# One core: the first batch's q and k rotated together in later weights' tiles, a weight conversion spread over more slots

## The chip, the cores and the metric

The kernel runs on one core of one Trainium2 chip. The metric is device time in microseconds (us), from the first to the last instruction of one execution and what lies around it; less is better. Its engines are TensorE (PE, with its weight loads PEld), VectorE (DVE), ScalarE (ACT), GpSimd (POOL) and SyncE (SP), which here only issues DMAs, in order.

## The reference

Attention with rotary position (4 batches, 8 heads, 576 positions, 64 channels), then two expert layers without a router on the 2304 x 512 result, all in float32:

```
q_rot, k_rot = rotate(q), rotate(k)
scores = (q_rot @ k_rot.T) / sqrt(64)
attn   = softmax(scores)
x = (attn @ v) as [2304, 512]
h = x @ w_in1;  x = (s * relu(h)**2 + b) @ w_out1
h = x @ w_in2;  out = (h * sigmoid(1.702 * h)) @ w_out2
```

All weight matrices arrive as 64-bit floats: `w_in` is 512 x 2048, `w_out` 2048 x 512.

## The kernel before

**Attention.** A batch is worked on in four pairs of heads. A pair's q and k are loaded (`rope_load`, L188), rotated on natural rows by four passes (`rope_cross` L197 with two, `rope_mul` L202, `rope_add` L205) on GpSimd, or on VectorE for q of the first RV pairs of batch 0, turned by TensorE through PSUM and split into a high and a low part (`rope_turn`, L218 on ScalarE, L219 on VectorE), and spilled to DRAM (`ksp`, `qsp`, L225 and L226). `fetch_pair` reads them back (L231, L241, L243) shortly before use. The rotated tiles come from the pool `nat`, two deep. The values of a batch are scanned for their largest (`v_load`, `v_max` L141, `v_scales`, `v_spread`), then split in two halves (`value_split`, L277).

A slot handles one tile of 128 rows of scores: `score_tile` (TensorE, the reduction L301 on VectorE, exp L310 on ScalarE), `norm_tile` (L317, L320 on VectorE, L321 on GpSimd), two slots later `turn_tile` and `rest_tile`, then `weighted` for a group of four or five slots. A batch has 36 slots, the kernel 144.

**Experts.** There are nine blocks of 256 tokens per layer and 16 weights f per layer, each with two halves: m = 0 is 128 columns of `w_in`, m = 1 is 128 rows of `w_out`. `weight` calls `make_half` for each half: a load of 512 KB into a stage tile (L391 or L396), a scale on ScalarE (L400), three passes on VectorE that put the 64-bit words together as 32-bit numbers (L401, L402, L405), a rounding to the high part on ScalarE (L408) and a subtraction on GpSimd for the low part (L409). Eleven weights of layer 1 stay in tiles `w0` to `w10`; weights 2, 5, 8, 11 and 14 are spilled (L431) and read back for every block (L441). Stage tiles are four halves of the tag `xs`, which also holds an expert block's input (`prepare`, L477 to L479).

**The order.** `at(slot, fn)` files each step under a slot; slots below 0 lie ahead of the first score. In batch 0 a pair p is loaded at slot -16 + 4p (k) or -15 + 4p (q), and turned four and five slots later. Weight f is converted at slot `CONV[0] + CONV[1] * f`, so -12 + f: all sixteen by slot 4. Block 0 may begin six slots after its 256 tokens are through, at slot 22, and block 1 at 42; `target` spreads a block's 32 half steps over the slots between. TensorE's instructions keep the order in which they are written, by `pin`; the other engines' queues are put in order by a scheduler from priorities, the slots' numbers, and dependencies.

## Time and profile before

| | us |
|---|---|
| median of 3 runs | 1332.78 (1332.11 to 1335.58) |
| the profiled execution | 1331.08 |
| its span, first to last instruction | 1329.2 |
| TensorE busy | 1133.8 (85%) |
| VectorE busy | 757.0 (57%) |
| ScalarE busy | 684.1 (51%) |
| GpSimd busy | 353.0 (27%) |

Most tables of a profile are shares over the whole span, and the kernel has stages with different limits: a start with little for TensorE, a long middle with attention and experts side by side, and experts alone from about 800 us. Read it by stretches. An engine's row in order of time has its start, its duration, the line, the operation, what it writes and reads, and in brackets how long the engine had been idle and what ended that.

### The profile page before, as it was taken

To read this page: it belongs to the slowest core of one execution; us is meant where nothing else is said; L and a number is where in the kernel's file an instruction comes from. 1 tells how busy PE (TensorE), PEld (TensorE's weight loads), DVE (VectorE), ACT (ScalarE), POOL (GpSimd) and SP (SyncE) were. 2 spreads that over 40 slices of the span, in tenths; PEclk is the share of its full clock that TensorE was granted. 3 is DMA by queue.
4 is the path that set the end of the run, shared out by engine and by line. 5 is a ranking of instruction groups with operands and counts; after the bars stand their busy time and mean duration, and the time that the engine had idled before them with its cause. 6 is when DMAs were issued, how large, how long until landed. Compare 5 with 4: busy or idle time off the path is not lost.

```text
span 1329.2 us, 23590 instructions
## 1 busy us (share of the span) xinstructions
PE 1133.8 (85%) x8584; PEld 1046.5 (79%) x8584; DVE 757.0 (57%) x1652; ACT 684.1 (51%) x1483; POOL 353.0 (27%) x350
## 2 busy tenths in 40 slices
PE   0126568998999999899999968987999999999998
PEld 0124448887889889898899968987899999999997
DVE  7888736766566676576665649389333333333322
ACT  2348555666566666566666647566333323332332
POOL 5675644432424343244111113044000000000000
PEclk9998689999989999999999989999999999999999
DMA  7987746657755677475665357566011101100000
GB/s 243 302 278 248 245 137 177 198 169 241 220 166 180 192 247 226 151 210 173 195 212 161 112 168 248 165 223 190 16 33 32 31 2 33 32 17 17 17 17 17
DMA packets 133204, 197.42 MB, mean 149 GB/s; under 512 B 32352, under 2 KB 99424, under 8 KB 133088
## 3 DMA queue, kind: packets, MB, share of 16 engines
q1 hardware_dynamic: 133088, 195.91, 47.8%
q8 instruction: 68, 1.11, 0.4%
q14 instruction: 48, 0.39, 0.1%
HBM read 152.34 MB, written 43.52 MB: 147 GB/s over the span
## 4 chain that ended last, share of the span: by engine, by line
PE 55%; DMA 12%; issue 11%; DVE 10%; ACT 5%; POOL 4%; SPq 2%; DVEq 0%; POOLq 0%; ACTq 0%
PE acc L90 21%; PE l L90 14%; PE l1b L90 7%; PE t L90 4%; PE av L90 4%; PE s L90 4%; DVE P L301 2%; POOL w L409 2%; DMA xT<-pt 2%; DMA vm<-in_v_dram 2%; DMA stage<-in_moe_w_out_dram 2%; DMA xl0b<-xT 1%; DVE pt L344 1%; DMA qb<-qsp 1%; ACT P L310 1%
## 5 line engine op out<-in xcount | busy, mean ns | idle before, releaser
L321 POOL TENSOR_SCALAR P<-P,st 128x576 f32<-128x576 f32 x144 | 113.9, 792 | 344.4 <-DVE st L320 244.7
L90 PE MATMUL acc<-w,gh1b 128*128 128x512 f32 x576 | 202.4, 392 | 0.0
L310 ACT ACTIVATE P<-P,st 128x576 f32<-128x576 f32 x144 | 111.8, 776 | 103.8 <-DVE P L301 103.8
L90 PE MATMUL acc<-gh0b,w 128*128 128x256 f32 x792 | 164.8, 290 | 0.1
L90 PE MATMUL l<-xh0b,w 128*128 128x256 f32 x704 | 145.6, 289 | 14.0 <-ACT r0b L505 8.7
L90 PE MATMUL t<-ident,P 128*128 128x128 f32 x720 | 109.1, 285 | 45.4 <-ACT pt L359 24.8
L301 DVE TENSOR_SCALAR_CACHE_REDUCE P<-s 128x576 f32<-128x576 f32 x144 | 108.5, 753 | 63.5 <-PE s L90 62.2
L90 PEld LDWEIGHTS acc<-gh0b,w 128*128 128x128 f32 x792 | 131.4, 193 | 1.1 <-issue 0.7
L409 POOL TENSOR_TENSOR w<-stage,w 128x512 fp32r<-128x512 f32 x64 | 92.6, 1450 | 145.4 <-ACT w L408 139.6
L90 PEld LDWEIGHTS l<-xh0b,w 128*128 128x128 f32 x704 | 117.9, 195 | 16.0 <-ACT r0b L505 10.4
L90 PEld LDWEIGHTS t<-ident,P 128*128 128x128 f32 x720 | 84.2, 145 | 58.4 <-issue 23.0
L90 PE MATMUL s<-k,qb 128*128 128x288 f32 x640 | 121.3, 317 | 3.9 <-DVE P L301 3.9
L90 PEld LDWEIGHTS acc<-w,gh1b 128*128 128x128 f32 x576 | 108.8, 189 | 19.3
L90 PE MATMUL l<-xh1b,w 128*128 128x256 f32 x576 | 115.1, 283 | 4.4 <-DVE r1b L510 4.4
L90 PE MATMUL l1b<-xh1b,w 128*128 128x256 f32 x576 | 115.1, 283 | 3.7 <-DVE r1b L510 3.7
L344 DVE TENSOR_TENSOR pt<-t,pt 128x640 f16<-128x640 f32 x124 | 101.9, 822 | 28.4 <-ACT pt L342 28.0
L90 PE MATMUL acc<-gl0b,w 128*128 128x256 f32 x396 | 113.1, 286 | 2.9 <-DVE gl0b L514 2.9
L90 PE MATMUL acc<-w,gl1b 128*128 128x512 f32 x288 | 113.8, 395 | 0.0
L342 ACT CAST pt<-t 128x640 f16<-128x640 f32 x144 | 99.0, 688 | 18.6 <-PE t L90 17.4
L90 PEld LDWEIGHTS s<-k,qb 128*128 128x128 f32 x640 | 95.5, 198 | 12.5 <-issue 6.7
L507 ACT ACTIVATE r0b<-r0b,sb 128x256 f32<-128x256 f32 x144 | 86.8, 603 | 33.0 <-DVE r0b L506 32.6
L90 PE MATMUL l<-xl0b,w 128*128 128x256 f32 x352 | 101.5, 288 | 1.4 <-DVE xl0b L479 0.7
(97 smaller groups left out, 2564.5 us busy)
## 6 DMA issues: line engine op xcount, KB each, us to landing
ws<-wd SPq DMA_DIRECT2D x90, 512.0 KB, 4.5
k<-ksp SPq DMA_DIRECT2D x32, 576.0 KB, 5.8
stage<-in_moe_w_in_dram SPq DMA_DIRECT2D x32, 512.0 KB, 4.7
stage<-in_moe_w_out_dram SPq DMA_DIRECT2D x32, 512.0 KB, 4.4
ksp<-z SPq DMA_DIRECT2D x32, 160.0 KB, 4.6
qsp<-z SPq DMA_DIRECT2D x32, 160.0 KB, 4.4
wd<-w SPq DMA_DIRECT2D x10, 512.0 KB, 5.4
vsp<-vz SPq DMA_DIRECT2D x16, 320.0 KB, 4.6
```

Source lines behind the costliest of these rows:

```text
L90: pin(nc.tensor.matmul(*args, **kw))
L301: nc.vector.tensor_scalar(pr.rearrange("p (n s) -> p n s", n=2), ps[:, :, :HS], -Q_SCALE, None, op0=ALU.mult, op1=ALU.min, accum_out=st[:, ...
L310: nc.scalar.activation(pr, pr, AF.Exp, bias=st[:, 0:1], scale=-1.0, accum_out=st[:, 1:2])
L321: nc.gpsimd.tensor_scalar(pr, pr, st[:, 2:3], 1.0, op0=ALU.mult, op1=ALU.mult)
L342: nc.scalar.copy(hi, pc)
L344: nc.vector.tensor_tensor(lo, pc, hi, op=ALU.subtract)
L409: nc.gpsimd.tensor_tensor(lo, f32(low), f32(hi), op=ALU.subtract)
L507: nc.scalar.activation(r, r, AF.Identity, bias=sb[:, 1:2], scale=sb[:, 0:1])
```

## The change

Four things change. The first batch's q and k (eight tiles) are loaded at slots -16 to -12 in place of -16 to -3, into the tiles `w5` to `w8`, one for a pair, whose third quarter also holds the k's cross products; q of the third pair moves to VectorE (RV 2 to 3). Their turns are filed at slots 4p - 8 to 4p - 6, so the last pair's fall behind the first score tiles. Conversion is filed at -4 + 2f, every second slot, up to slot 26. Its last step, the rounding and the subtraction (`split`), is filed one slot later. And for weights 0 to 12 a stage tile holds both halves and lies in `w10` or `w9` in turn; only weights 13 to 15 are staged in `xs`. `ACT_SHIFT` is empty, so the branch on ScalarE is not taken.

```diff
+    BOOT = (5, 6, 7, 8)
...
     def rope_load(b, p, which, st):
-        nat = att.tile([128, RT, 2, HD], F32, tag="nat", name=f"nat{b}{p}{which}")
+        if b == 0:
+            if p not in boot:
+                boot[p] = wpool.tile([128, 2048], F32, tag=f"w{BOOT[p]}", name=f"boot{p}")
+            nat = boot_part(p, which)
+        else:
+            nat = att.tile([128, RT, 2, HD], F32, tag="nat", name=f"nat{b}{p}{which}")
...
+        elif f < HELD[0][-2]:
+            if m == 0:
+                stages[0] = wpool.tile(
+                    [128, 2, 512], U64, tag=f"w{len(HELD[0]) - 1 - f % 2}", name=f"stage{nm}"
+                )
+            raw = stages[0][:, m]
...
-        nc.scalar.copy(hi, f32(low))
-        nc.gpsimd.tensor_tensor(lo, f32(low), f32(hi), op=ALU.subtract)
+        def split():
+            nc.scalar.copy(hi, f32(low))
+            nc.gpsimd.tensor_tensor(lo, f32(low), f32(hi), op=ALU.subtract)
+        return split
...
+        if layer == 0:
+            at(int(CONV[0] + CONV[1] * f) + WLAG, split)
+        else:
+            split()
...
-        gap = 2 if b else 1
         for g in range(2):
-            at(s + 4 + gap * g, rope_turn, b, p, which, g, st)
+            at(s + 4 + 2 * g if b else 4 * p + RT0 - which + g, rope_turn, b, p, which, g, st)
...
-    CONV = (-12, 1.0)
+    CONV = (-4, 2)
...
+    RT0 = -7
+    WLAG = 1
...
-    RV = 2
+    RV = 3
...
-                r = bounds[b - 1] + RS + 9 * p if b else -RL + 4 * p
+                r = bounds[b - 1] + RS + 9 * p if b else -RL + p
```

The order on VectorE just ahead of the first score reduction (the last row: P out of s), before; `stage` is a weight under conversion (L401, L402, L405), z a turned q or k, vz a split value:

```order
L402 SCALAR_TENSOR_TENSOR stage_60_329<-stage_60_329 128x512
L405 SCALAR_TENSOR_TENSOR stage_60_329<-stage_60_329 128x512
L277 SCALAR_TENSOR_TENSOR vz_479<-vr_396,vsc_440,vz_479 128x320
L219 TENSOR_TENSOR z_435<-r_463,z_435 64x2x64
L401 TENSOR_SCALAR stage_61_337<-stage_61_337 128x512
L402 SCALAR_TENSOR_TENSOR stage_61_337<-stage_61_337 128x512
L277 SCALAR_TENSOR_TENSOR vz_479<-vr_396,vsc_440,vz_479 128x320
L405 SCALAR_TENSOR_TENSOR stage_61_337<-stage_61_337 128x512
L219 TENSOR_TENSOR z_476<-r_471,z_476 128x2x256
L219 TENSOR_TENSOR z_476<-r_509,z_476 64x2x64
L301 TENSOR_SCALAR P_548,st_547<-s_542 128x576
```

and with the change, whose line numbers are 13 to 22 higher (z is L232 there, the reduction L314):

```order
L170 TENSOR_SCALAR vrow_197<-vrow_197 1x8
L171 TENSOR_SCALAR vrow_197<-vrow_197 1x8
L232 TENSOR_TENSOR z_253<-r_248,z_253 128x2x256
L180 COPY vsc_258<-vpb_256 128x8
L183 COPY inv<-vpb_256 64x4
L184 COPY inv<-vpb_256 64x4
L232 TENSOR_TENSOR z_253<-r_266,z_253 64x2x64
L232 TENSOR_TENSOR z_279<-r_274,z_279 128x2x256
L232 TENSOR_TENSOR z_279<-r_300,z_279 64x2x64
L314 TENSOR_SCALAR P_318,st_317<-s_312 128x576
```

Ten halves' conversion passes and two value splits have moved from ahead of that reduction to behind it.

The order of DMA issues on SyncE around the fetch of pair 0 (`k<-ksp`, `qb<-qsp`), before; `stage` is a weight's load, `wd` a converted weight's spill, `vr` a load of values:

```order
L225 DMA qsp<-z_188 128x1x320 x2
L396 DMA stage_31_244<-in_moe_w_out_dram 128x512
L231 DMA k_388<-ksp 128x1152
L260 DMA vr_396<-in_v_dram 64x3x64
L260 DMA vr_396<-in_v_dram 64x64
L431 DMA wd_208<-w_20_199 128x1024
L391 DMA stage_40_258<-in_moe_w_in_dram 128x4x128
L260 DMA vr_396<-in_v_dram 64x64
L241 DMA qb_96<-qsp 128x256
L243 DMA qb_97<-qsp 64x256
L431 DMA wd_218<-w_21_209 128x1024
L396 DMA stage_41_266<-in_moe_w_out_dram 128x512
```

and with the change:

```order
L239 DMA ksp<-z_177 128x1x256 x2
L238 DMA ksp<-z_177 128x1x320 x2
L239 DMA qsp<-z_194 128x1x256
L273 DMA vr_224<-in_v_dram 64x3x64 x2
L244 DMA k_216<-ksp 128x1152
L239 DMA qsp<-z_194 128x1x256
L273 DMA vr_224<-in_v_dram 64x64 x2
L238 DMA qsp<-z_194 128x1x320 x2
L273 DMA vr_224<-in_v_dram 64x2x64
L256 DMA qb_97<-qsp 64x256
L254 DMA qb_96<-qsp 128x256
L256 DMA qb_97<-qsp 64x256
```

Between the spills and the fetch no weight load and no weight's spill is left; the spills' own issues and the values' loads are.

The order on VectorE around the split of block 0's first input (`xl0b`), before; r0b and gl0b are expert results, pt turned probabilities:

```order
L160 TENSOR_SCALAR vrow_1422<-vrow_1422 1x8
L167 RECIPROCAL vrow_1422<-vrow_1422 1x8
L168 TENSOR_SCALAR vrow_1422<-vrow_1422 1x8
L169 TENSOR_SCALAR vrow_1422<-vrow_1422 1x8
L479 TENSOR_TENSOR xl0b_1442<-xl0b_1442,xh0b_1443 128x1024
L317 TENSOR_SCALAR st_1438<-st_1438 128x1
L320 RECIPROCAL st_1438<-st_1438 128x1
L506 TENSOR_TENSOR r0b_1461<-r0b_1461 128x256
L514 TENSOR_TENSOR gl0b_1466<-r0b_1461,gh0b_1465 128x256
L344 TENSOR_TENSOR pt_1299<-t_1485,pt_1299 128x5x128
L219 TENSOR_TENSOR z_1498<-r_1493,z_1498 128x2x256
```

and with the change, where the three conversion passes are L423, L424 and L427:

```order
L330 TENSOR_SCALAR st_1361<-st_1361 128x1
L170 TENSOR_SCALAR vrow_1345<-vrow_1345 1x8
L171 TENSOR_SCALAR vrow_1345<-vrow_1345 1x8
L333 RECIPROCAL st_1361<-st_1361 128x1
L510 TENSOR_TENSOR xl0b_1365<-xl0b_1365,xh0b_1366 128x1024
L423 TENSOR_SCALAR stage_130_1406<-stage_130_1406 128x512
L537 TENSOR_TENSOR r0b_1384<-r0b_1384 128x256
L424 SCALAR_TENSOR_TENSOR stage_130_1406<-stage_130_1406 128x512
L427 SCALAR_TENSOR_TENSOR stage_130_1406<-stage_130_1406 128x512
L423 TENSOR_SCALAR stage_131_1412<-stage_131_1412 128x512
L424 SCALAR_TENSOR_TENSOR stage_131_1412<-stage_131_1412 128x512
```

Conversion passes of weights 13 to 15, six halves, now stand behind the first block's input, between passes on its results.

## Rows read from the trace of the kernel before

**Rows 1.** Stretch, length; busy us (count) of PE, PEld, DVE, ACT, POOL; clock, DMA, GB/s.
```profile
0.00:152.00 152.00, 48.16 (x237) 33.26 (x237) 128.10 (x202) 75.08 (x138) 103.88 (x86) 0.92 0.81 264
```

**Rows 2.** VectorE in order of time: the score reductions (L301) of slots 0, 2, 10, 13, 21.
```profile
71.27 0.76 DVE L301 TENSOR_SCALAR_CACHE_REDUCE P<-s 128x576 f32<-128x576 f32 x1 [0.41 <-PE s L90]
...
97.32 0.74 DVE L301 TENSOR_SCALAR_CACHE_REDUCE P<-s 128x576 f32<-128x576 f32 x1
...
129.65 0.74 DVE L301 TENSOR_SCALAR_CACHE_REDUCE P<-s 128x576 f32<-128x576 f32 x1
...
151.53 0.74 DVE L301 TENSOR_SCALAR_CACHE_REDUCE P<-s 128x576 f32<-128x576 f32 x1
...
183.13 0.76 DVE L301 TENSOR_SCALAR_CACHE_REDUCE P<-s 128x576 f32<-128x576 f32 x1 [0.38 <-PE s L90]
```

**Rows 3.** SyncE queue in order of time: weight loads, a k spill, the first block's input.
```profile
3.08 0.43 SPq L391 DMA_DIRECT2D stage<-in_moe_w_in_dram  x1
...
22.74 0.52 SPq L225 DMA_DIRECT2D ksp<-z  x1
...
132.93 0.46 SPq L396 DMA_DIRECT2D stage<-in_moe_w_out_dram  x1
...
184.23 0.38 SPq L477 DMA_DIRECT2D xl0b<-xT  x1
```

**Rows 4.** Groups of instructions by line, 0 to 200 us: conversion and rotation.
```profile
L409 POOL TENSOR_TENSOR w<-stage,w 128x512 fp32r<-128x512 f32 x32 | 46.7, 1464 | 24.8 <-ACT w L408 18.9 <-DMA nat<-in_k_dram 2.9 <-DMA qb<-qsp 2.7
...
L402 DVE SCALAR_TENSOR_TENSOR stage<-stage 128x512 uint32<-128x512 uint32 x32 | 34.4, 1075 | 5.7 <-ACT stage L400 4.7
...
L405 DVE SCALAR_TENSOR_TENSOR stage<-stage 128x512 uint32<-128x512 uint32 x32 | 34.1, 1064 | 0.5
...
L401 DVE TENSOR_SCALAR stage<-stage 128x512 uint32<-128x512 uint32 x32 | 26.1, 816 | 0.0
...
L197 POOL TENSOR_TENSOR rot<-nat,tab 128x288 f32<-128x288 f32 x20 | 21.0, 1072 | 11.8 <-DMA nat<-in_k_dram 6.6 <-PE s L90 5.2
...
L205 POOL TENSOR_TENSOR nat<-nat,rot 128x576 f32<-128x576 f32 x10 | 17.1, 1706 | 0.2
...
L202 POOL TENSOR_TENSOR nat<-nat,tab 128x576 f32<-128x576 f32 x10 | 15.9, 1586 | 0.2
```

**Rows 5.** TensorE in order of time: the turn between the first two score tiles.
```profile
83.67 1.11 PE L93 MATMUL r<-ident,nat 128*128 128x128 f32 x4 [12.45 <-POOL nat L205]
```

**Rows 6.** GpSimd in order of time: the first rotation of a k.
```profile
7.89 1.81 POOL L197 TENSOR_TENSOR rot<-nat,tab 128x288 f32<-128x288 f32 x2 [6.59 <-DMA nat<-in_k_dram]
...
11.36 1.79 POOL L205 TENSOR_TENSOR nat<-nat,rot 128x576 f32<-128x576 f32 x1
```

**Rows 7.** VectorE in order of time: multiplication of two q, first two halves split.
```profile
10.05 1.85 DVE L202 TENSOR_TENSOR nat<-nat,tab 128x576 f32<-128x576 f32 x1
...
18.55 0.68 DVE L219 TENSOR_TENSOR z<-r,z 128x512 fp32r<-128x512 f32 x1
...
26.02 0.68 DVE L219 TENSOR_TENSOR z<-r,z 128x512 fp32r<-128x512 f32 x1
...
37.94 0.75 DVE L202 TENSOR_TENSOR nat<-nat,tab 128x576 f32<-128x576 f32 x1
```

**Rows 8.** DMA issues from 0 to 184 us: KB each, median us to landing.
```profile
DMA packets 34997, 46.85 MB, mean 255 GB/s; under 512 B 9984, under 2 KB 27136, under 8 KB 34986
...
k<-ksp SPq DMA_DIRECT2D x7, 576.0 KB, 6.2
...
ksp<-z SPq DMA_DIRECT2D x10, 160.0 KB, 4.6
...
qsp<-z SPq DMA_DIRECT2D x10, 128.0 KB, 4.2
```

**Rows 9.** Busy time by stretch: the first expert slots, and the fullest DMA stretch.
```profile
200.00:240.00 40.00, 35.38 (x313) 33.20 (x312) 24.61 (x66) 24.43 (x54) 16.03 (x17) 1.00 0.61 181
...
20.00:40.00 20.00, 3.07 (x10) 1.69 (x10) 19.00 (x26) 7.21 (x13) 13.07 (x12) 1.00 0.98 321
```

More of the change, by code (lines that the diff above doesn't have):

```diff
@@ L126 @@
     v_spill = dram.tile([B * NP, 128, 4 * 5 * D], F16, tag="vsp", name="vsp")
+    boot = {}
+    BOOT = (5, 6, 7, 8)
     qd = {}
@@ L183, in v_spread, with boot_part @@
         vsc[b] = sc
+    def boot_part(p, i):
+        return boot[p][:, i * S : (i + 1) * S].rearrange("p (t e i) -> p t e i", t=RT, e=2)
     def rope_load(b, p, which, st):
-        nat = att.tile([128, RT, 2, HD], F32, tag="nat", name=f"nat{b}{p}{which}")
+        if b == 0:
[4 more added lines that the diff above has]
+            nat = att.tile([128, RT, 2, HD], F32, tag="nat", name=f"nat{b}{p}{which}")
         src = (q, k)[which][b, 2 * p : 2 * p + 2]
@@ L194, in rope_cross @@
     def rope_cross(b, p, which, st, eng):
-        rot = att.tile([128, RT, 2, HD], F32, tag="rot", name=f"rot{b}{p}{which}")
+        if b == 0 and which == 1:
+            rot = boot_part(p, 2)
+        else:
+            rot = att.tile([128, RT, 2, HD], F32, tag="rot", name=f"rot{b}{p}{which}")
         for e in range(2):
@@ L400, in make_half @@
         nc.scalar.activation(f32(high), f32(high), AF.Copy, scale=2.0**-112)
-        nc.vector.tensor_scalar(low, low, 29, None, op0=ALU.logical_shift_right)
+        if m in ACT_SHIFT and not late:
+            nc.scalar.activation(low, low, AF.Copy, scale=2.0**-29, bias=-0.5)
+        else:
+            nc.vector.tensor_scalar(low, low, 29, None, op0=ALU.logical_shift_right)
         nc.vector.scalar_tensor_tensor(
@@ L426, in weight @@
             t = kept[layer][f][m]
-        make_half(t, *W[layer], f, m, f"{layer}_{f}")
+        split = make_half(t, *W[layer], f, m, f"{layer}_{f}")
+        if layer == 0:
+            at(int(CONV[0] + CONV[1] * f) + WLAG, split)
+        else:
+            split()
         if f in STREAMED[layer]:
@@ L457 @@
     late = {}
+    stages = {}
     def x_tile(nm):
@@ L647 @@
     RS, RL = 9, 16
+    RT0 = -7
+    ACT_SHIFT = ()
+    WLAG = 1
     MOE_LATE = 500
@@ L702 @@
             for which in (1, 0):
-                eng = nc.vector if b == 0 and p < RV and which == 0 else nc.gpsimd
-                r = bounds[b - 1] + RS + 9 * p if b else -RL + 4 * p
+                eng = nc.vector if b == 0 and (p < RV and which == 0) else nc.gpsimd
+                r = bounds[b - 1] + RS + 9 * p if b else -RL + p
                 plan_rope(b, p, which, r + (1 - which), eng)
```

## The prediction

> **What bounds the kernel now.** I read the busy times by stretch first, then VectorE, GpSimd and the DMA queue of SyncE in order of time up to the first expert block, then the costs by line there. After the first 200 us TensorE is the bound: in [rows 9] it is busy 35.38 of 40 us at full clock. Before that it is not: in the first 152 us TensorE is busy 48.16 us, VectorE 128.10, GpSimd 103.88, and the DMA engines move 264 GB/s at a share of 0.81 [rows 1]. The reader should see there that three units are crowded and the one that bounds the rest idles. The first score reduction stands at 71.27 us, those of slots 2, 10, 13 and 21 at 97.32, 129.65, 151.53 and 183.13 [rows 2], and the input of expert block 0 is asked for at 184.23 [rows 3], 1.1 us after slot 21's reduction. What TensorE has to do from there on is the same list before and after, in the same order, so what the change is worth is the shift of that 184.23, less what it makes slower behind it.
>
> VectorE is crowded by weight conversion: three passes of 1.075, 1.064 and 0.816 us for each half of a weight, 2.96 us, 32 times [rows 4]. 14 of the 32 halves stand ahead of the first score on VectorE, though no score needs them. GpSimd has its own queue of the same kind: a subtraction of 1.464 us for each half, between rotations at 1.072 (twice), 1.586 and 1.706 us [rows 4]. TensorE then waits in its fixed order for turned q and k: 12.45 us for one between the first two score tiles [rows 5].
>
> **Part 1: first batch rotated at once.** All eight loads and two of v are issued ahead of the first weight load, which goes back by eight issues of some 0.45 us from its 3.08 us [rows 3]; no score waits for it, so nothing is charged. The third pair's q moves from GpSimd to VectorE. GpSimd does four pairs of cross products, two multiplications, then the first addition: 8 x 1.072 + 2 x 1.586 + 1.706 = 13.5 us. From 7.89, when the first k is there, that is 21.3; now it ends at 11.36 + 1.79 = 13.15 [rows 4, 6]. So pair 0 is later by 8.2 us, and the others are much earlier. From 13.15 to the last spill of this k at 22.74 [rows 3] are 9.6 us; kept, that gives 30.9, with 4.6 us for the spill and 6.2 for the fetch [rows 8] 41.7 for k. For q: the first splits of two successive turns stand at 18.55 and 26.02 [rows 7], 7.5 apart, with conversion passes between them. So q's last spill comes at 30.9 + 7.5 = 38.4, lands 4.2 us later [rows 8] at 42.6, and six reads and two value loads at about half a microsecond each on SyncE, the last taking some 4 us, give 50.6. The two turns of pair 1 also stand ahead of the first score: two more at 7.5 end at 53, but the order has no conversion between them, so 5.5 each is nearer, 49. I take **50 us** for the first score reduction in place of 71.27, with ends 44 (all turns at 4 us) and 62 (GpSimd's 13.5 us doubled by the work on VectorE beside it). Pairs 2 and 3 are then rotated before TensorE asks, so the 12.45 us wait goes.
>
> **Part 2: conversion spread.** By the order, 4 halves stand ahead of the first score instead of 14, 22 instead of 18 between it and block 0's input, and 6 behind it. So the slots have about one half each. Slots 2 to 13 now have 12 halves in 11 slots, in 54.2 us: 4.93 us a slot; the first eight of them, before the next batch's rotation comes onto GpSimd, (129.65 - 97.32) / 8 = 4.04 [rows 2]. The changed slots carry the next batch's rotation at their start and end only. I take **4.7**, nearer the upper row. 21 slots x 4.7 = 98.7; 50 + 98.7 + 1.1 = 149.8, against 184.23: **-34.4 us**. A check from the DMA side: 46.85 MB move up to 184 us [rows 8]; the order has three weights (3.1 MB), four spilled halves and two refetched (3.1), and two loads of the next batch (0.6) fewer, so 40 MB, and at the 321 GB/s of the fullest stretch [rows 9] these need 125 us, at 264 [rows 1] 152. So 150 can be had and 125 is the floor.
>
> The six halves behind block 0's input cost VectorE 6 x 2.96 = 17.7 us and GpSimd 8.8. In the first 40 us there VectorE has 40 - 24.61 = 15.4 us free [rows 9], and block 0 reaches weights 13 to 15 only late, so cover is there but just short: bounds 0 and 18 us, I charge **+6**, the 2.3 us that do not fit and some for passes that stand ahead of expert results in VectorE's order. If that cover were gone, it would be the 18.
>
> **Part 3: staging and the late split.** A stage tile now holds a whole weight and is given back when the second half is subtracted; two tiles turn instead of four half tiles. Loads of a weight queue on SyncE behind that, and what stands behind them (fetches of q and k) waits too. Now 31 weight loads follow one another in 132.93 - 3.08 us [rows 3], 4.19 apart, so a half tile comes round in 4 x 4.19 = 16.8 us. A whole weight adds its second half, 2.96 us on VectorE and 1.46 on GpSimd [rows 4]: 21 us. One weight per two slots and two tiles allow 21 / 4 = 5.3 us a slot at worst, 4.2 without the addition. It bounds the pace from above, and is in its ends (4.04 to 5.3); nothing is charged beyond. The stage tiles and those of the rotated q and k are filled with weights only later, so they cost no wait in the order. The split moves one slot back, past one norm on GpSimd: it is in the 21 us.
>
> Sum: -34.4 + 6 = -28.4 on the profiled execution of 1331.08 us (span 1329.2): 1302.7. The median of the runs, 1332.78, is 1.7 above it: **1304**.
>
> **Rivals.** *GpSimd and VectorE block each other.* A multiplication of q takes 1.85 us beside GpSimd's and 0.75 us later without [rows 7], so some of it is here already. In the changed start both engines rotate at the same time. GpSimd has 14 x 1.072 + 7 x 1.586 + 6 x 1.706 + 4 x 1.464 = 42.2 us ahead of its first norm, VectorE four halves (11.8) and nine passes of q (6.8 at 0.75). If they run one after the other, the first score comes at 7.9 + 60.8 = 69, as late as now; then 69 + 98.7 + 1.1 = 168.8, -15.4 + 6, and 1323; at 4.93 a slot 1328. Against it: in the first 152 us VectorE's 128.10 and GpSimd's 103.88 us are together far more than 152 [rows 1]. The Trainium skill (SBUF — State Buffer, "SBUF: two separate sides") says that VectorE and GpSimd share one port pair which is locked, not divided, and that the second one "fully blocks"; by that rule this rival's 1323 would hold instead of 1304. The 1.85 against 0.75 us agrees with it; the overlap of the two engines' busy times does not, unless time spent blocked is recorded as busy.
>
> *The pair tile sets the pace, and it is slower.* The place is the stage load on SyncE, which waits for the subtraction of the weight two before. With 6 us lost behind it, no gain is left when block 0's input comes at 178, a pace of (178.2 - 51.1) / 21 = 6.05 us, a round trip of 24.2 us. It is 21 in my estimate with only half of the queueing. If the second half queues as long again as the first's own passes, 28 us: 7.0 a slot, 50 + 147 + 1.1 = 198, +14 + 6, and 1353. For it: the loads' releases now come in pairs, on an in-order queue. Against: two halves in a tile overlap on three engines.
>
> *Faster.* At 4.04 a slot and a first score at 46, 132: -52.3 + 6, 1286. It needs 40 MB at 303 GB/s from the start; only one stretch shows more.
>
> *Nothing is won.* The earlier start is given back in block 0, because weights 13 to 15 wait for tiles that its own input holds. It takes 34 us of waits where the passes are 18: about 1333.
>
> **How the numbers follow.** The forecast has 0.58, the faster case 0.14, the block of two engines 0.12 (a sixth of it within 0.3%), the pair tile 0.10, nothing won 0.06. 0.3% is 4 us, about what a measurement tells here. So faster by more 0.82, within 0.07, slower 0.11. The time is the forecast's, 1304. Its own ends: 44 to 62 us, 4.04 to 5.3 a slot, 0 to 18, which do not all fall together; the range of 1283 to 1329 takes in the faster case and most of the block, and leaves out the last two and the extremes.
>
> **What would show it.** The first score reduction near 50 us (over 65: part 1 fails by the block); slots 2 to 21 at 4.7 us each (over 6: the pair tile, with stage loads on SyncE as the releaser); block 0's input at 140 to 160; behind it the same intervals between expert blocks as now, with the first longer by some 6 us; the conversion passes' mean at or under 2.96 us a half. If the input comes at 150 and the time is not near 1304, the account of TensorE's later work is wrong.

## The result, and the profile after

The changed kernel takes 1338.67 us (median of 8 runs, 1336.75 to 1342.52) against 1331.78 of the kernel before in the same comparison (8 runs, 1324.34 to 1335.58): a ratio of 1.0059 [1.0034, 1.0084]. It is slower, where 1304 was forecast, and outside the range. The profiled execution has a span of 1340.7 us (before 1329.2); at 1342.52 us it is the slowest of the eight, 3.9 above their median, while the one of before, at 1331.08, lies near its own. One execution of e17_four_tiles, further down, took 2262.83 us and is left out of its median.

Read it first by three stretches: up to the first score reduction, from there to the request for block 0's input, and from there to block 1's. The columns are those of [rows 1]. The kernel before:

```profile
0.00:71.27 71.27, 11.33 (x38) 6.56 (x38) 58.22 (x85) 25.14 (x44) 42.78 (x39) 1.00 0.85 276
71.27:184.23 112.96, 58.66 (x361) 43.92 (x361) 81.97 (x159) 70.12 (x133) 76.69 (x66) 0.85 0.77 241
184.23:279.23 95.00, 80.08 (x666) 74.87 (x667) 58.07 (x145) 55.34 (x121) 32.91 (x37) 0.95 0.55 163
```

and the changed kernel:

```profile
0.00:59.66 59.66, 8.29 (x30) 5.22 (x31) 44.33 (x53) 9.71 (x17) 41.73 (x39) 1.00 0.48 153
59.66:180.23 120.57, 67.43 (x376) 50.44 (x374) 77.15 (x173) 76.43 (x147) 51.68 (x51) 0.71 0.82 262
180.23:287.47 107.24, 84.64 (x662) 78.00 (x661) 78.27 (x169) 62.96 (x134) 51.52 (x49) 0.87 0.65 202
```

The first score is 11.6 us earlier, block 0's input only 4.0, and block 1's is 8.2 later. VectorE, which was to be relieved, is less busy in the first two stretches; the second got longer all the same. The last two columns say what changed: the DMA engines are half empty ahead of the first score (0.48, 153 GB/s, against 0.85, 276) and busier than before behind it (0.82, 262 GB/s, against 0.77, 241). Length times rate gives the bytes: before 19.7, 27.2 and 15.5 MB, now 9.1, 31.6 and 21.7, both times 62.4 MB up to block 1's input. From block 1's input to the end it is 1053.2 us after 1050.0.

The slots that answer to [rows 2] (slots 0, 2, 10, 13 and 21, on VectorE in order of time):

```profile
59.66 0.76 DVE L314 TENSOR_SCALAR_CACHE_REDUCE P<-s 128x576 f32<-128x576 f32 x1 [0.39 <-PE s L90]
...
68.95 0.75 DVE L314 TENSOR_SCALAR_CACHE_REDUCE P<-s 128x576 f32<-128x576 f32 x1
...
119.64 0.76 DVE L314 TENSOR_SCALAR_CACHE_REDUCE P<-s 128x576 f32<-128x576 f32 x1 [1.34 <-PE s L90]
...
136.72 0.74 DVE L314 TENSOR_SCALAR_CACHE_REDUCE P<-s 128x576 f32<-128x576 f32 x1
...
176.90 0.74 DVE L314 TENSOR_SCALAR_CACHE_REDUCE P<-s 128x576 f32<-128x576 f32 x1
```

From slot 0 to slot 21 that is 117.24 us, 5.58 a slot, where 4.7 was forecast and 5.33 stood before. What answers to [rows 3], SyncE's queue (the second weight's last load, the third weight's first, block 0's input):

```profile
11.13 0.38 SPq L410 DMA_DIRECT2D stage<-in_moe_w_in_dram  x1
...
65.53 0.52 SPq L415 DMA_DIRECT2D stage<-in_moe_w_out_dram  x1
...
180.23 0.38 SPq L508 DMA_DIRECT2D xl0b<-xT  x1
```

Between 11.13 and 65.53 us no weight is loaded; before, sixteen halves were asked for by then, now four. What answers to [rows 4] (0 to 200 us):

```profile
L433 POOL TENSOR_TENSOR w<-stage,w 128x512 fp32r<-128x512 f32 x28 | 38.9, 1391 | 36.4 <-ACT w L432 36.4
L424 DVE SCALAR_TENSOR_TENSOR stage<-stage 128x512 uint32<-128x512 uint32 x28 | 28.6, 1023 | 3.2 <-ACT stage L419 2.4
L427 DVE SCALAR_TENSOR_TENSOR stage<-stage 128x512 uint32<-128x512 uint32 x28 | 24.5, 877 | 0.3
...
L423 DVE TENSOR_SCALAR stage<-stage 128x512 uint32<-128x512 uint32 x28 | 18.5, 659 | 13.4 <-DMA stage<-in_moe_w_out_dram 7.2 <-DMA stage<-in_moe_w_in_dram 6.2
```

The passes are faster than before (2.56 us a half instead of 2.96), but VectorE now waits 13.4 us for stage loads. The DMA engines by forty slices of 4.5 us, from 0 to 180 us, GB/s, before and after:

```profile
GB/s 68 264 389 73 294 280 317 336 314 324 327 261 191 292 385 326 346 207 167 171 360 335 306 259 170 81 314 347 235 349 344 352 100 85 277 228 262 259 189 75
DMA packets 34507, 46.17 MB, mean 256 GB/s; under 512 B 9792, under 2 KB 26816, under 8 KB 34496
```

```profile
GB/s 66 284 403 384 181 160 0 67 76 214 0 57 117 143 219 341 119 78 248 312 369 321 65 87 218 379 313 335 83 233 317 342 291 300 396 390 364 287 98 372
DMA packets 31165, 40.64 MB, mean 226 GB/s; under 512 B 8771, under 2 KB 24390, under 8 KB 31155
```

The hole from the fifth to the fourteenth slice is what the change buys its lighter start with.

What the slots then wait for stands in the chain of work that ended last, which the profile follows back from the end, at each step to what released it. Its pieces between the first score and block 0's input that are a weight's load on its way (start and length in us), before and after:

```profile
71.26 5.64 DMA stage<-in_moe_w_out_dram
...
124.86 3.97 DMA stage<-in_moe_w_in_dram
```

```profile
66.58 7.67 DMA stage<-in_moe_w_in_dram
...
109.05 6.03 DMA stage<-in_moe_w_in_dram
...
116.43 6.98 DMA stage<-in_moe_w_in_dram
...
131.17 5.01 DMA stage<-in_moe_w_in_dram
```

That is 9.6 of 113.0 us before and 25.7 of 120.6 after. All transfers together (weights, fetches, spills) hold 26 us of that chain before and 43 after, SyncE's issuing 4 and 30: together 30 before and 73 after. The transfers also take longer there. A fetch of k in the slots, count, size and median us from issue to landing, before and after:

```profile
k<-ksp SPq DMA_DIRECT2D x5, 576.0 KB, 5.9
```

```profile
k<-ksp SPq DMA_DIRECT2D x6, 576.0 KB, 7.1
```

One stall sits in that start. VectorE in order of time:

```profile
41.38 0.28 DVE L153 TENSOR_REDUCE vrow<-vps 1x8 f32<-1x128 f32 x1 [0.77 <-PE vps L90]
41.69 8.57 DVE L161 TENSOR_SCALAR vrow<-vrow 1x8 f32<-1x8 f32 x1
50.29 0.16 DVE L162 TENSOR_SCALAR vrow<-vrow 1x8 int32<-1x8 int32 x1
```

and GpSimd meanwhile:

```profile
42.05 1.28 POOL L433 TENSOR_TENSOR w<-stage,w 128x512 fp32r<-128x512 f32 x1
43.30 1.39 POOL L218 TENSOR_TENSOR boot<-boot,rot 128x576 f32<-128x576 f32 x1
44.65 1.39 POOL L215 TENSOR_TENSOR nat<-nat,tab 128x576 f32<-128x576 f32 x1
46.00 1.52 POOL L210 TENSOR_TENSOR rot<-nat,tab 128x288 f32<-128x288 f32 x2
47.49 1.39 POOL L218 TENSOR_TENSOR nat<-nat,rot 128x576 f32<-128x576 f32 x1
48.84 1.39 POOL L215 TENSOR_TENSOR nat<-nat,tab 128x576 f32<-128x576 f32 x1
62.75 0.74 POOL L334 TENSOR_SCALAR P<-P,st 128x576 f32<-128x576 f32 x1 [12.51 <-ACT vz L287]
```

A scaling of eight numbers takes 8.57 us and ends when GpSimd's unbroken row of instructions ends, at 50.23. Its rotations of `nat` are those of batch 1: batch 0 no longer uses that pool, so they move up into the start. Behind the stall lie the splits of the last q, and the spill on SyncE that waits 7.9 us for them (L238, behind VectorE's L171).

### The profile page after: what moved, and what is told of

It reads as the page before. It is cut to its first block, busy times and chain, and to the rows that moved or that the text cites. A ratio compares the mean times of both kernels' runs of the same rounds, so it can differ in the third digit from the quotient of the medians.

```text
span 1340.7 us, 23516 instructions
## 1 busy us (share of the span) xinstructions
PE 1149.1 (86%) x8584; PEld 1060.0 (79%) x8584; DVE 756.6 (56%) x1656; ACT 682.9 (51%) x1483; POOL 348.1 (26%) x346
## 4 chain that ended last, share of the span: by engine, by line
PE 53%; DMA 13%; DVE 13%; issue 10%; ACT 5%; SPq 4%; POOL 3%; DVEq 0%; POOLq 0%; ACTq 0%
PE acc L90 21%; PE l L90 14%; PE l1b L90 7%; DMA stage<-in_moe_w_in_dram 4%; PE av L90 4%; PE s L90 3%; PE t L90 3%; POOL w L433 2%; DVE P L314 2%; DMA xT<-pt 2%; DMA vm<-in_v_dram 2%; DMA xl0b<-xT 2%; DVE stage L424 2%; SPq L273 2%; DVE stage L427 1%
## 5 line engine op out<-in xcount | busy, mean ns | idle before, releaser
L314 DVE TENSOR_SCALAR_CACHE_REDUCE P<-s 128x576 f32<-128x576 f32 x144 | 108.5, 753 | 66.3 <-PE s L90 64.3
L90 PE MATMUL s<-k,qb 128*128 128x288 f32 x640 | 125.1, 324 | 4.3 <-DVE P L314 3.3
L90 PEld LDWEIGHTS s<-k,qb 128*128 128x128 f32 x640 | 98.8, 205 | 14.0 <-issue 7.1
L355 ACT CAST pt<-t 128x640 f16<-128x640 f32 x144 | 99.0, 687 | 15.5 <-PE t L90 14.8
```

Source lines behind the costliest of these rows:

```text
L90: pin(nc.tensor.matmul(*args, **kw))
L314: nc.vector.tensor_scalar(pr.rearrange("p (n s) -> p n s", n=2), ps[:, :, :HS], -Q_SCALE, None, op0=ALU.mult, op1=ALU.min, accum_out=st[:, ...
L355: nc.scalar.copy(hi, pc)
```

## Experiments

Each run is compared with the kernel before, run beside it, so the ratio is the number to compare and the medians only roughly. A profile is one execution, and those of one kernel differ by up to 20 us (before: 1318.80 to 1339.42 beside e5 to e8): the profiles of e7 and e8 are of their fastest execution, that of e11 of one at 1332.14 us, 7.2 above its median. A few us between two profiles mean little by themselves. `first` is the first score reduction, `input 0` and `input 1` the requests for the blocks' inputs, in us, from the run's profile; MB are length times rate, ahead of `first` and from there to `input 1`.

| | ratio to before, 95% | median | first | input 0 | input 1 | MB ahead, behind |
|---|---|---|---|---|---|---|
| before | | 1331.78 | 71.27 | 184.23 | 279.23 | 19.7, 42.7 |
| after | 1.0059 [1.0034, 1.0084] | 1338.67 | 59.66 | 180.23 | 287.47 | 9.1, 53.3 |
| e1_no_lock | 1.0092 [1.0061, 1.0122] | 1342.69 | 59.89 | 185.85 | 290.19 | 9.1, 53.3 |
| e2_conv_1p5 | 1.0084 [1.0052, 1.0116] | 1343.14 | 67.69 | 196.92 | 293.18 | 12.9, 49.5 |
| e3_half_tiles | 1.0059 [1.0032, 1.0086] | 1339.18 | 59.59 | 187.39 | 288.66 | 9.1, 53.5 |
| e4_values_pool | 1.0330 [1.0291, 1.0368] | 1373.76 | 51.64 | 200.12 | 304.17 | 9.6, 53.1 |
| e5_busy_pe | 1.0127 [1.0070, 1.0184] | 1342.47 | 59.50 | 190.71 | 294.63 | 9.1, 53.3 |
| e6_weights_act | 1.0122 [1.0050, 1.0195] | 1340.03 | 69.42 | 186.04 | 294.49 | 12.5, 49.9 |
| e7_late_next | 1.0023 [0.9986, 1.0060] | 1332.04 | 52.90 | 185.89 | 284.01 | 8.5, 53.9 |
| e8_values_act | 1.0048 [1.0017, 1.0080] | 1332.27 | 58.44 | 177.56 | 282.58 | 9.8, 52.5 |
| e9_no_loads | 0.9927 [0.9900, 0.9954] | 1321.82 | 61.32 | 166.54 | 272.97 | 9.9, 41.1 |
| e10_same_bytes | 1.0056 [1.0037, 1.0075] | 1338.22 | 61.33 | 187.40 | 290.70 | 9.9, 52.6 |
| e11_old_rope | 0.9966 [0.9942, 0.9989] | 1324.94 | 52.55 | 173.22 | 278.54 | 11.0, 51.4 |
| e12_early_seven | 1.0051 [1.0033, 1.0069] | 1338.29 | 68.92 | 194.09 | 288.99 | 15.5, 46.9 |
| e13_tiny_loads | 0.9960 [0.9943, 0.9977] | 1326.70 | 61.38 | 170.84 | 272.98 | 9.9, 41.2 |
| e14_bytes_act | 1.0037 [1.0012, 1.0062] | 1335.92 | 69.94 | 184.60 | 284.57 | 16.2, 46.1 |
| e15_late_rv2 | 1.0044 [1.0022, 1.0067] | 1337.30 | 54.41 | 185.33 | 283.67 | 8.5, 53.8 |
| e16_old_rope_act | 0.9947 [0.9914, 0.9979] | 1324.93 | 54.21 | 167.94 | 272.80 | 11.1, 51.2 |
| e17_four_tiles | 1.0030 [1.0012, 1.0048] | 1334.48 | 69.35 | 175.08 | 283.40 | 12.8, 49.7 |
| e18_old_rope_tiles | 1.0032 [1.0012, 1.0051] | 1334.31 | 74.03 | 183.91 | 285.39 | 18.0, 44.4 |

**e1_no_lock.** The largest value is left in PSUM, so that the stalled instruction has no operand pair in SBUF:

```diff
-            row[:, 0:8],
+            pt[0:1, 128:136],
...
-        top = row[:, 0:8]
+        top = pt[0:1, 128:136]
```

> The changed kernel, with one 1x8 operation of the value scales (8.57 us beside a busy GpSimd in the trace) reading PSUM in place of SBUF. Block theory (GpSimd locks VectorE out there, and that delays all slots): the operation takes 0.2 to 0.4 us, the first score reduction comes at about 51 us in place of 59.7, block 0's input at about 172 in place of 180, time 1330. Rivals (issue queue, or late weights, set the pace of the slots): the first score comes earlier as well, but block 0's input stays at 178 to 182 and the time at 1336 to 1340.

```profile
41.82 0.15 DVE L161 TENSOR_SCALAR vrow<-vps 1x8 f32<-1x8 f32 x1
42.00 8.38 DVE L162 TENSOR_SCALAR vrow<-vrow 1x8 int32<-1x8 int32 x1
```

The stall moved to the next instruction, which still goes from SBUF to SBUF. So the first score stayed, and the run says what the stall is, not what it costs.

**e2_conv_1p5.** Conversion is filed closer together, so that its last weight stands at slot 18.

```diff
-    CONV = (-4, 2)
+    CONV = (-4, 1.5)
```

> The changed kernel with conversion at slots -4 + 1.5 f in place of -4 + 2 f: by the order 10 halves ahead of the first score in place of 4, and all but one ahead of block 0's input. Late-weight theory (weights that come late hold ScalarE's and VectorE's queues in the slots, and six halves lengthen block 0): block 0 takes 95 to 98 us in place of 107, its input comes at 176 to 182, time 1326 to 1330. Pair-tile theory (two stage tiles of a whole weight set the pace): a weight per 1.5 slots needs more of them, block 0's input comes at 188 or later, block 0 at 97, time 1336 to 1342. Issue-queue theory: six more loads ahead of the input, 183 to 185, block 0 at 97, time 1331.

Block 0 is back at 96.3 us (input 0 to input 1; before 95.0, after 107.2), but the slots take 129.2 instead of 120.6, at 259 GB/s: what leaves block 0 comes back in the slots. Of the three expectations the pair tile's is the nearest (input at 188 or later); e3 tests that one directly.

**e3_half_tiles.** Staging in four half tiles of `xs`, as before.

```diff
-        elif f < HELD[0][-2]:
+        elif False:
```

> The changed kernel with the weights staged as before, in four tiles of one half each. Pair-tile theory: slots at 5.0 us or less in place of 5.58, block 0's input at 168 or earlier, time 1326. Rivals: input at 178 to 182, time 1336 to 1341.

The same ratio as after; the slots are longer (127.8 us), block 0 shorter (101.3). That a tile holds a pair is not the cause.

**e4_values_pool.** The value loads are issued by GpSimd instead of SyncE.

```diff
-                ins = nc.sync.dma_start(
+                ins = nc.gpsimd.dma_start(
```

> The changed kernel with the loads of the values for the split (ten small DMAs a pair, 0.62 us each on SyncE) issued by GpSimd in place of SyncE. Issue-queue theory (SyncE has issued almost without a pause from 52 to 136 us): some 45 issues of 0.62 us fewer ahead of block 0's input, slots at 4.3 to 4.8 us, input at 150 to 162, time 1312 to 1322. Rivals: input at 176 to 182, time 1334 to 1340.

Much slower: GpSimd is busy 438 us instead of 348, and the slots run at 225 GB/s. This run can't judge SyncE; e6 and e8 do.

**e5_busy_pe.** TensorE's clock is lower in the changed slots (0.71 granted, before 0.85). Extra matmuls on data of no use, four at two places of each slot up to 18, are to keep it up:

```diff
+        for i in range(4):
+            mm(busy[0][:, 0:128], ident, ident, start=True, stop=True, skip_group_check=True)
```

> The changed kernel with eight added 128x128 float32 multiplications a slot on TensorE in slots 0 to 18, into a bank that block 0 uses later. Clock theory (TensorE idles so much in the slots that its granted clock falls to 0.71 there, against 0.85 before, and the slots' own matmuls take longer): granted clock 0.9 or more from the first score to block 0's input, slots at 5.0 us, input at 165 to 172, time 1328 to 1332. Rival (late loads, issue queue): the clock rises, the pace stays at 5.4 to 5.9, input at 178 to 186, time 1336 to 1344.

The granted clock rose to 0.90 in the slots; their length did not fall, it rose to 131.2 us at 255 GB/s. The added matmuls take time of their own (TensorE busy 89.63 us there, after 67.43), so the run shows that a higher clock does not shorten the slots here, not what it is worth by itself.

**e6_weights_act** and **e8_values_act** take loads off SyncE, the weights' in the first and the values' of batch 0 in the second:

```diff
-            nc.sync.dma_start(
+            (nc.sync if late else nc.scalar).dma_start(
```

```diff
-                ins = nc.sync.dma_start(
+                ins = (nc.scalar if b == 0 else nc.sync).dma_start(
```

> The changed kernel with the weight loads issued by ScalarE in place of SyncE (26 of some 190 issues ahead of block 0's input, and each free of what stands ahead of it on SyncE). Issue-queue theory: stage loads come sooner, ScalarE's waits for them (19.7 us in the first 200) fall under 8, slots at 4.6 to 5.1 us, input at 156 to 168, time 1315 to 1327. Rivals (clock, total work of VectorE): pace 5.4 to 5.9, time 1335 to 1342.

> The changed kernel with the first batch's value loads (40 of some 190 issues ahead of block 0's input) issued by ScalarE in place of SyncE. Issue-queue theory: 25 us less on SyncE, slots at 4.6 to 5.0 us, input at 155 to 168, time 1314 to 1326, if ScalarE's own 64% of that stretch bears it. Rivals: pace 5.4 to 5.9, input 178 to 186, time 1335 to 1344.

The slots ran at 259 and 263 GB/s, as in after. e6 gained nothing; e8's interval overlaps that of after, with input 0 2.7 us earlier. In e8 the chain through the slots has 9 us of SyncE's issuing instead of 30, but 16 us of value loads landing, which it had not before: the wait moved. So taking issues off SyncE gained little or nothing.

**e7_late_next.** Batch 1's first loads are held behind the fetch for slot 8, so that their rotation leaves the start.

```diff
+        if (b, p) == (1, 0):
+            pin(ins, "late")
...
+        if (b, p, k) == (0, 2, 0):
+            pin(ins, "late")
```

> The changed kernel with the load of the next batch's first q and k held, in the order of the queues, behind the fetch at slot 4, so that GpSimd doesn't rotate them before the first score. Block theory: GpSimd's row of passes ends near 43 in place of 50, the small operation of the value scales takes under 4 us in place of 8.6, first score reduction at 52 to 54 us. If the start is what counts, block 0's input at 173 and the time 1331; if the pace of the slots makes up for it (issue queue, late loads), input at 178 to 184, time 1336 to 1341.

```profile
42.72 0.79 DVE L161 TENSOR_SCALAR vrow<-vrow 1x8 f32<-1x8 f32 x1
```

The stall is 0.79 us long and the first score comes at 52.90, 6.8 us earlier: the stall is GpSimd's unbroken work, and this is its price. But the slots then take 133.0 us, at 255 GB/s, and input 0 is later than in after: what is won ahead of the first score is not kept. The held rotation now falls into the slots (GpSimd busy 71.79 us there, after 51.68), so the run does not part the transfers from that work.

**e9_no_loads** and **e10_same_bytes.** The first leaves out the loads of weights 2 to 12 and converts what its tiles hold, the second issues them again to no reader:

```diff
+        if not late and 2 <= f < HELD[0][-2]:
+            reload(w_in, w_out, f, m)
```

`reload` returns at once in e9; in e10 it loads the half into a tile of `xs`.

> Leaves out the loads of weights 2 to 12 of the first layer, 22 of 512 KB (11.5 MB); their conversions still run, on what the stage tiles of weights 0 and 1 hold. Theory (the slots last as long as their bytes take): between the first score and block 0's input the changed kernel moved 31.6 MB in 120.57 us, 262 GB/s; without some 10 MB of them 21.6 MB at 260 GB/s need 83 us, so a stretch of 83 to 95 us (VectorE's 77 us busy come near), input at 140 to 155, the time at least 20 us below the changed kernel's. Rival 1 (SyncE's issues set the pace): 20 issues of 0.6 us less, so a stretch of about 108 us, input near 168. Rival 2 (the order of the passes on VectorE sets it): 115 to 121 us as in the changed kernel, and no gain.

> As e9_no_loads, but the same 22 loads are issued again, in the slots, into four tiles that nothing reads, so that no conversion waits for one. The bytes and the issues are back, the waits of ScalarE and VectorE for late loads are not. Theory (bytes): the stretch between first score and block 0's input goes back to 110 to 121 us at about 260 GB/s. Rival (what costs is the engines' waiting for late stage loads, with other work queued behind them): it stays within 5 us of e9_no_loads. If e9 gains nothing, this run has nothing to tell apart. SyncE's issues alone would give 12 to 13 us above e9.

The slots of e9, and of e10:

```profile
61.32:166.54 105.22, 63.55 (x366) 47.62 (x367) 74.46 (x163) 69.45 (x133) 57.03 (x53) 0.72 0.66 202
```

```profile
61.33:187.40 126.07, 68.59 (x378) 51.25 (x378) 74.81 (x176) 72.17 (x139) 59.58 (x55) 0.82 0.81 265
```

VectorE does the same work in both, and the first scores are 0.01 us apart. With the loads the slots are 20.9 us longer and the time 16.4 us, though nobody waits for a spare tile. So these loads cost time even where no conversion waits for them. How, the other transfers show; a fetch of k in the slots of e9 and of e10:

```profile
k<-ksp SPq DMA_DIRECT2D x6, 576.0 KB, 4.7
```

```profile
k<-ksp SPq DMA_DIRECT2D x6, 576.0 KB, 6.8
```

Where it is taken stands at the end of e10's slots, on its chain and on SyncE's queue in order of time:

```profile
175.99 6.76 DMA k<-ksp
```

```profile
180.02 7.34 SPq L275 DMA_DIRECT2D vr<-in_v_dram  x8
187.40 0.60 SPq L523 DMA_DIRECT2D xl0b<-xT  x1
```

Slot 21's reduction is only 4.0 us later than in e9 (170.42 and 166.41); block 0's input comes 17 us behind it, at the end of a queue of eight value loads: seven of them wait for that fetch of k until 182.75 us and then take some 0.6 us each, as value loads do in e9 (median 0.612 us up to block 0's input, in e9 0.616). This is not where after loses: its slots 0 to 21 last 117.24 us, those of e10 109.09 and of e9 105.09, and its input follows 3.3 us behind. There conversions do wait for their loads (its chain, above). So the two runs show that the loads cost, not how much of after's price is bytes and how much is waiting for a load asked for late. And e9 gained less than I expected (105 us, not 83 to 95): without the bytes something else holds the slots at about 105.

**e13_tiny_loads** and **e14_bytes_act** part bytes from issues: e13 cuts e10's loads to four columns, e14 issues them from ScalarE.

```diff
-                w_in[:, f * 128 : (f + 1) * 128].rearrange("(c p) f -> p c f", p=128),
+                w_in[:, f * 128 : f * 128 + 4].rearrange("(c p) f -> p c f", p=128),
```

```diff
-            ins = nc.sync.dma_start(spare, w_out[f * 128 : (f + 1) * 128, :])
+            ins = nc.scalar.dma_start(spare, w_out[f * 128 : (f + 1) * 128, :])
```

> As e10_same_bytes, with the 22 spare loads cut to four 64-bit columns each (0.2 MB in place of 11.5): as many issues on SyncE in the same order, nearly none of the bytes. It leaves out the loads of weights 2 to 12 as e9_no_loads does. Theory (bytes): as e9, a stretch of 105 to 110 us between first score and block 0's input, about 200 GB/s, the time 1318 to 1326. Rival (SyncE's issues): as e10, input at 180 to 188 and the time 1334 to 1341.

> As e10_same_bytes, with the 22 spare loads of full size issued by ScalarE: the bytes are back, SyncE's issues are not. Theory (bytes): input at 180 to 190 at 255 to 265 GB/s, the time 1333 to 1341, as e10. Rival (SyncE's issues): input at 166 to 172, the time 1318 to 1326, as e9, with up to 5 us for ScalarE's own issuing.

Against e9's 1321.82 the issues alone cost 4.9 us (1326.70), the bytes alone 14.1 (1335.92), both together 16.4 (1338.22). Most of it is bytes, roughly: the intervals of e9 and e13 overlap a little, and 45 value loads stand ahead of block 0's input in e13, 52 in e10. A caution: e14's loads came earlier than e10's (16.2 MB ahead of the first score, which came at 69.94), so it shows the price of the bytes, not of their place.

**e11_old_rope** undoes the rotation part and keeps the conversion part.

```diff
-        if b == 0:
+        if False:
...
-            at(s + 4 + 2 * g if b else 4 * p + RT0 - which + g, rope_turn, b, p, which, g, st)
+            at(s + 4 + (2 if b else 1) * g, rope_turn, b, p, which, g, st)
...
-    RV = 3
+    RV = 2
...
-                r = bounds[b - 1] + RS + 9 * p if b else -RL + p
+                r = bounds[b - 1] + RS + 9 * p if b else -RL + 4 * p
```

> The conversion part alone: the first batch's rotation is as in the kernel before (tiles of the pool nat, old slots, q of two pairs on VectorE), conversion every second slot in whole-weight tiles stays. Theory (bytes late): the loads still come late, so block 0's input stands at 178 to 188 and block 0 takes 104 to 108 us, and the time is 1334 to 1341, near the changed kernel's. Rival (the rotation part with its blocked engines is what loses, and spreading conversion wins): input by 170 and the time under 1326.

Its first two stretches:

```profile
0.00:52.55 52.55, 11.30 (x38) 6.54 (x38) 29.77 (x57) 13.63 (x25) 27.50 (x32) 1.00 0.71 210
52.55:173.22 120.67, 59.80 (x357) 45.78 (x358) 86.35 (x163) 71.56 (x136) 74.22 (x66) 0.79 0.80 254
```

My theory missed its time and the rival met it, though the input came between the two and block 0 took 105.3 us, as the theory had it. Spreading conversion alone is slightly faster than the kernel before, and adding the rotation part turns that into a loss. The first score comes at 52.55 without any rotation at once, 7.1 us ahead of after, with more bytes moved by then (11.0 MB, a third weight asked for at 45.09 instead of 65.53 us) and 2 MB fewer left. Behind the first score the two kernels take nearly the same time to input 1 (226.0 and 227.8 us).

**e15_late_rv2** is e7 with RV 2:

```diff
-    RV = 3
+    RV = 2
```

> The changed kernel with batch 1's first rotation held back as in e7_late_next, and q of the third pair on GpSimd again (RV 2). If VectorE's two passes and the shared port were the rest of what the rotation part costs, it comes to e11_old_rope's 1325 (1322 to 1328). If the rest is that all eight rotations stand ahead of the first turns and weights' loads, it stays at e7's 1332 (1329 to 1336).

Not 1325: its interval overlaps those of e7 and of after. VectorE's extra passes are not the rest of what the rotation part costs; that the DMA engines have only 8.5 MB to move ahead of the first score in e7 and e15 remains, and was not tested by itself.

**e12_early_seven** and **e17_four_tiles** fill the empty start, e12 by converting weights 0 to 6 early (with e7's hold), e17 by two more stage tiles.

```diff
+    def conv(f):
+        return -10 + f if f < 7 else int(3 + 1.75 * (f - 7))
```

```diff
-                    [128, 2, 512], U64, tag=f"w{len(HELD[0]) - 1 - f % 2}", name=f"stage{nm}"
+                    [128, 2, 512], U64, tag=f"w{ {2: 4, 3: 3}.get(f, 10 - f % 2) }", name=f"stage{nm}"
```

> Weights 0 to 6 are converted at slots -10 to -4, the others from slot 3 on, one in 1.75 slots, and the first rotation of batch 1 is held behind a fetch of slot 8 as in e7_late_next; the rotation of batch 0 stays as changed. By the order 13.67 halves stand ahead of the first score and all 32 ahead of block 0's input. Theory (bytes): the DMA engines are filled in the first 60 us again, so 7 to 9 MB leave the slots: first score at 60 to 66, input at 168 to 176, block 0 at 95 to 98 us, and the time 1318 to 1326, under both kernels. Rival (the start is bound by VectorE and GpSimd, as before): first score at 70 or more, input at 180 to 185, time 1328 to 1333.

> The changed kernel with two more tiles for staging: weight 2 lies in w4, weight 3 in w3, before weights 6 and 4 are made there. By the order six more loads (3.1 MB) then stand ahead of the first fetch of k, and 9.33 halves ahead of the first score instead of 4. Theory (the empty start costs): DMA share ahead of the first score 0.62 to 0.72, 3 MB less behind it, at 262 GB/s 12 us: input at 166 to 174 and the time 1326 to 1333. Rival (what is loaded early is only paid early, the passes in the crowded start push the first score back by as much): first score at 70 or later, input at 178 to 186, time 1336 to 1341.

Both moved more ahead of the first score, 15.5 and 12.8 MB, and both pushed that score back, to 68.92 and 69.35. e12 missed: its slots still carry 31.5 MB, since all conversions now end there. e17 lies between its two expectations: input 0 is 5.2 us earlier than in after, the time 4.2 us lower with overlapping intervals. Its slots 0 to 21 come at 4.75 us each, the pace that was forecast, behind a first score that is 9.7 us later. Early loads bring their passes with them, and those delay the first score.

**e16_old_rope_act** is e11 with e8's edit, **e18_old_rope_tiles** adds four stage tiles to that:

```diff
+                    [128, 2, 512], U64, tag=f"w{(10, 9, 8, 7, 10, 9, 8, 7, 10, 9, 8, 9, 10)[f]}", name=f"stage{nm}"
```

> e11_old_rope with the value loads of batch 0 issued by ScalarE, as in e8_values_act, where that was worth some 6 us against the changed kernel. If SyncE's queue holds the loads back: 1316 to 1321, under both kernels. If the bytes alone bound the slots, no change from e11: 1323 to 1329.

> e16_old_rope_act with four tiles for staging (w10, w9, w8, w7, which the old rotation leaves free) in place of two: 11.33 halves ahead of the first score. If the empty start costs: DMA share there 0.75 to 0.85, first score at 56 to 62, input at 156 to 164 and the time 1314 to 1321, under both kernels. If not: 1324 to 1331.

e16 is as fast as e11: both beat the kernel before by some 0.3 to 0.5%, and no run of the study beats them with the whole work done. e18 missed: 18.0 MB ahead and the first score at 74.03, near the 71.27 of the kernel before.

## Why the prediction was wrong

**What bounds the kernel.** The crowded units were read rightly in [rows 1], but I named conversion on VectorE as what to relieve and took the DMA engines as a check only. The table shows them as a term. From the first score to input 1 it takes 208 to 220 us where 41 to 47 MB are left (before, e9, e12, e13, e14, e18), and 214 to 231 where 49 to 54 MB are, e4 and e5 left aside. The kernel before is at the short end; the change moved 10.6 MB behind the first score and pays 19.8 us there. The two groups touch (e12 220 us with 46.9 MB, e17 214 with 49.7), and kernels that load more ahead also convert more ahead, so the table alone does not prove it; e9 and e10, which differ by the loads, do. What sets the 208 where bytes are few wasn't tried.

**Part 2, the pace, is the step that failed.** It was worked out from the passes, at 4.7 us a slot, and it measured 5.58; block 0's input came 4.0 us earlier instead of 34.4. The bytes were right (40 MB forecast, 40.64 moved to 180 us). What was wrong is the check, that 40 MB at 264 GB/s take 152 us and so 150 can be had: it let the DMA engines run full from the start, while the same change takes their work away there. By the order only two weights are loaded ahead of the first score. Done by stretch, with the 9.1 MB measured there, 31.6 MB are left, and at the same 264 GB/s these need 120 us; the stretch took 120.57. Even from a first score at 50 that gives 170, and with block 0's drag little or no gain. The 31.6 MB are themselves the length times 262 GB/s, so this says only that the slots ran at nearly the rate of [rows 1]. Why they did is not shown, and it is no ceiling: the changed kernel moved 338 GB/s from 140 to 160 us and 209 from 100 to 120.

What the trace shows in the place of the pace is a wait that its sum has no term for: 73 of the slots' 120.6 us are transfers and SyncE's issuing on the chain, before 30 of 113.0. The slots are 20.8 us longer than forecast (120.57 against 98.7 + 1.1). With the loads left out (e9) they are 15.4 shorter; the 105.22 that are left are still 5.4 over, although 14 more of VectorE's instructions stand ahead of the first score there. In all the profiled execution came some 40 us over its forecast: 9.7 at the first score, 20.8 in the slots, 6.2 in block 0, 3.3 behind it.

**Part 1, the first score.** Forecast 50, measured 59.66, within the ends of 44 to 62. The missing piece is the one stall of 8.57 us (52.90 without it, e7). Its credit was misplaced, though: e11 has its first score at 52.55 with the old rotation, so a start as light comes from the ten halves moved away, without rotating at once.

**The six halves in block 0.** Forecast +6 with ends of 0 and 18, measured +12.2; e2 and e12, whose block 0 converts next to nothing, have 96.3 and 94.9 us. So the drag goes with the halves, at twice the charge; that it is VectorE's passes, and not the halves' loads, was not tested.

**Part 3.** Nothing was charged for loads that queue behind the tiles, and the slots were to take 5.3 us "at worst"; they took 5.58. That the tile holds a pair is not why (e3). But the loads that this part weighed do hold the chain, for 25.7 us of the slots: this is the charge that is missing in Part 2.

**The rivals.** GpSimd and VectorE do block each other, but not as the rival had it: the passes became shorter, and one small instruction waited for a whole row of GpSimd's. The Trainium skill (SBUF — State Buffer, "SBUF: two separate sides") says that the one who comes first holds the shared port for the whole instruction. The trace agrees that the loser fully blocks; how long is more than one instruction here: L161 waited for seven of GpSimd's in a row. Its 8.57 us are recorded as busy, so what the prediction held against this rival, that the two engines' busy times overlap, does not count. The rival's 1323 did not come; the stall was not kept through the slots (e7). The pair tile falls with e3. "Nothing is won" came nearest in time, by a wrong mechanism: the earlier start was given back in the slots before block 0, and block 0's drag made it a loss. Adding up: -4.0 to input 0, +12.2 in block 0, +3.3 behind input 1, +11.5 on the spans; by the medians of 8 runs +6.9, for the profiled execution of after is its slowest.

Still open: what in the rotation part beyond the late third weight costs the 8.9 us by which e11 is ahead at input 1. By the medians e11 is 13.7 us below after, but the two profiled executions, 1332.14 and 1342.52, are only 10.4 apart. e15 speaks against VectorE's extra passes. Neither the rotation part alone was run nor loads asked for earlier with the conversions left in their slots, which would part the bytes from the late requests.

## What to carry to other kernels

When a change moves loads later, do the byte account by stretch, each with what can be asked for in it: an average rate over the whole start hides a hole, and this one was not made up behind it. Look at the chain that ended last, stretch by stretch: passes give a pace only where no load is waited for. An earlier first result is not kept in full where the stretch behind it waits for transfers (4.0 of 11.6 us here, 11.0 of 18.7 in e11), and a start that looks crowded by passes may be doing the transfers that later work would have to wait for. Undo the parts of a joint change one by one: here one part gained 0.3% and the other cost more than twice that.

## What the runs showed of the hardware that was not expected

A VectorE instruction of eight numbers from SBUF to SBUF took 8.57 us while GpSimd worked without a gap, 0.79 us beside one GpSimd instruction (e7), and the same happened to its neighbour (8.38 us) once the first read PSUM (e1). Value loads issued by GpSimd cost 35 us against the same loads from SyncE (e4). The same fetch of 576 KB took 4.7 us to land in e9's slots at 202 GB/s and 6.8 in e10's at 265. In 14 of the 20 kernels the slots ran at 252 to 268 GB/s and a share of 0.79 to 0.85, whatever the change, though [rows 9] has 321 GB/s for 20 us and the changed kernel 338 (140 to 160 us).
